# A transformer block on one core: the written order kept for TensorE, VectorE and ScalarE to the end of the kernel

## The chip, the cores and the metric

The kernel runs on one core of a Trainium2 chip. A core has five instruction streams that run side by side and wait for each other by semaphores: TensorE (PE: matmuls; its weight loads are listed as PEld), VectorE (DVE), ScalarE (ACT), GpSimd (POOL) and SyncE (SP), which here only issues DMAs. Each stream executes its instructions in the order in which they stand. The metric is the device time of one execution in microseconds (us).

## The reference

The input is one sequence of 2048 rows of 640 floats. An attention block is followed by a gated MLP whose gate mixes rows:

```python
h  = x + _A_ref(_layernorm(x), wqkv, wo)     # 32 heads of 20, window of 256 rows
z  = gelu(layernorm(h) @ w_in)               # 640 -> 1728
z1 = z[..., :864]
z2 = layernorm(z[..., 864:])
g  = einsum("ts,bsf->btf", w_sp, z2) + b_sp  # 2048 x 2048 matrix over the rows
h2 = h + (z1 * g) @ w_out                    # 864 -> 640
```

All is float32. The kernel keeps that precision on TensorE by splitting each operand into a high part and a low rest and adding three products.

## The kernel before

The sequence is cut into 16 tiles of 128 rows. After attention, whose part of the program ends at line 657, the kernel goes through these stages:

1. **Output projection** (`for i in range(NT)`, 16 tiles). `norm_o` (L148, DVE) divides the attention output by the softmax sums, `split_o` (L156 a copy on ACT, L157 a subtraction on POOL) splits it, `proj_o` (L91, PE, 30 matmuls) multiplies it by `wo`, L1160 (DVE) adds the input, `layernorm` takes statistics (L75, L76 on DVE), the power on POOL (L77, L78), and scales on DVE (L81). `turn_h` (L806) transposes the result two tiles later. The sums come from `inverse_sums` (L348, a reciprocal on DVE of what a DMA, L345, has loaded). Meanwhile `win1_prep` splits the first half of `w_in` a few pieces per tile: copies on ACT (`zl<-wraw`), subtractions on DVE and POOL.
2. **z1**: eight `z_pair`s of 8 products each (L866), with Strassen-like sums of operands, so seven products in place of eight.
3. **z2, first half**: four `z2_pair`s, two tiles each, four products of 15 matmuls (L917). After the gelu on ACT (L921) come statistics on DVE (L939, L941), the power on POOL (L942, L943), the scaling on DVE (L947), and `right_blocks`: sums and splits of four blocks into seven pieces (`ze`, `zl`), high parts by ACT (L681), low parts by DVE and POOL (L675, the line of the helper `plus`).
4. **First gates**: eight `gate_pair`s of 7 products of 12 matmuls (L1013) of `w_sp` with the seven pieces of all four pairs; `w_sp` tiles are loaded into `fx` and split into `aw`.
5. **z2, second half**, and 6. **second gates**: the same with the other half of the rows; in the second gates each product is followed by transposes (L1041) and the last projection (L1052) of earlier tiles, and `w_out` is loaded and split in the first two of them (L124, L125).

Stages 2 to 6 are written as a list `steps`, one product each, and a table `later` of work that `at(n, f)` hangs on a step. `run(n)` emits, in this order, what hangs on step n, the product of step n, and the reading of its bank:

```python
    def run(n):
        for f in later.pop(n, []):
            f()
        if 0 <= n < len(steps):
            steps[n][0]()
            steps[n][1]()
```

Buffers are written out: four PSUM banks with the tag `a` and four with `b`, four rows, two halves of `fx`.

What sets the order of instructions on an engine is the scheduler of the framework, which by default reorders each engine's instructions as far as data allow, by its own estimate of when each would be ready. A context, `manual_schedule(engines=...)`, holds the listed engines to the order in which the program emits them. It is entered at the top for PE, DVE and ACT and held in the stack `ms`; line 657, `ms.close()`, leaves it. So in the kernel before attention runs in the written order, and all that follows in the scheduler's. POOL is never held; SP is held only inside a part of attention.

Of the kernel before, what the change touches and what calls it, by code (L numbers as in the profile page):

```python
# [34 lines left out]
def block_kernel(ctx, tc, x, wqk, wv, wo, w_in, wsp, bsp, w_out, out):  # L35
    nc = tc.nc
    ms = ctx.enter_context(ExitStack())
# [616 lines left out]
                pass  # L654


    ms.close()
    psK = ctx.enter_context(ExitStack())

    def acc_tile(name):  # L660
# [555 lines left out]
```

## Time and profile before

| | us |
|---|---|
| median of 3 runs | 1148.1 |
| lowest and highest | 1143.98, 1149.98 |
| span of the profiled execution | 1144.7 |

The profile page gives the profiled execution by its span, 3.4 us under the median. In what follows a row of the timeline gives start, duration, engine, line, operation, output and inputs, count, and in brackets the idle time before it with what ended it; a row of the windows gives, for a stretch of the span, the busy time of each engine (instructions in brackets), the granted clock of TensorE (1.00 is full) and the share of DMA. A row of groups gives busy time and mean ns of one, then the idle time before. The busy time of PE counts pipelined matmuls, so a busy PE at half clock looks as busy as at full clock; rates are therefore taken from start to start.

### The profile page before, as it was taken

Reading aid. Unit: us, or ns where it says so; the run is one execution under the profiler, and the core shown is the slowest. Engines: PE = TensorE matmul, PEld = TensorE weight load, DVE = VectorE, ACT = ScalarE, POOL = GpSimd, SP = SyncE. Lnnn points to the kernel's source line nnn. Section 1 sums busy time; section 2 is a strip of 40 time slices with the busy share of each in tenths; the row PEclk is TensorE's granted clock in tenths of the full one; section 3 lists DMA queues with packets and bytes.
Section 4 is the critical chain, followed back from the end, with each engine's and each line's share of the span. In section 5 each row is a group of like instructions: output and inputs, shape, how many; then the busy total and the mean of one; then the engine's idle time right before and its main releaser. Section 6 shows DMA issues by size and latency. Waiting matters only on the chain. (4 is left out here: it accounts for less than half of the span.)

```text
span 1144.7 us, 27633 instructions
## 1 busy us (share of the span) xinstructions
PE 1096.0 (96%) x10652; PEld 983.2 (86%) x10652; DVE 746.7 (65%) x1963; ACT 535.8 (47%) x1165; POOL 405.5 (35%) x553
## 2 busy tenths in 40 slices
PE   6999999999999999888999998999999899999998
PEld 6998887668788786788999997999999799999998
DVE  5541113789999996599677588455558974556543
ACT  3333433259999899344266554333334421222210
POOL 4124444547777678376220263000126410000000
PEclk9999999999999999899999998999999999999999
DMA  6212565656666635588455411323331463344322
GB/s 196 70 36 94 169 217 175 211 185 196 203 203 215 200 119 181 177 273 280 181 178 179 164 59 38 102 102 124 123 112 53 162 214 117 122 145 136 107 71 80
DMA packets 83844, 170.84 MB, mean 149 GB/s; under 512 B 11008, under 2 KB 47360, under 8 KB 79872
## 3 DMA queue, kind: packets, MB, share of 16 engines
q1 hardware_dynamic: 81408, 163.83, 44.3%
q10 hardware_dynamic: 2304, 5.24, 1.2%
q8 instruction: 83, 1.36, 0.5%
q14 instruction: 49, 0.40, 0.1%
HBM read 112.37 MB, written 56.23 MB: 147 GB/s over the span
## 5 line engine op out<-in xcount | busy, mean ns | idle before, releaser
L369 ACT ACTIVATE pt<-bank 128x384 f32<-128x384 f32 (+2 forms) x512 | 201.6, 496 | 13.9 <-PE bank L366 10.2
L1013 PE MATMUL g<-zl,aw 128*128 128x432 f32 x768 | 174.4, 362 | 7.3 <-ACT zl L681 4.9
L681 ACT ACTIVATE aw<-fx 128x512 fp32r<-128x512 f32 (+2 forms) x160 | 92.7, 595 | 187.6 <-PE g L1013 120.7
L312 DVE CUSTOM_DVE_ANT_0 junk<-bank,strip 128x288 bf16<-128x288 f32 x392 | 157.3, 454 | 6.6 <-PE bank L300 3.7
L1013 PEld LDWEIGHTS g<-zl,aw 128*128 128x128 f32 x768 | 144.8, 189 | 16.3 <-ACT zl L681 5.9
L1013 PE MATMUL g<-ze,aw 128*128 128x432 f32 x576 | 138.1, 368 | 6.0 <-DVE row L675 3.8
L675 DVE TENSOR_TENSOR aw<-fx,aw 128x512 fp32r<-128x512 f32 (+2 forms) x152 | 108.6, 723 | 37.2 <-ACT aw L681 36.7
L394 PE MATMUL pv<-pt,v_sb 128*32 128x192 f32 (+3 forms) x1984 | 126.8, 322 | 4.2 <-POOL pt L371 2.4
L1013 PEld LDWEIGHTS g<-ze,aw 128*128 128x128 f32 x576 | 109.2, 192 | 13.8 <-issue 3.2
L366 PE MATMUL bank<-slot 123*32 123x288 bf16 (+6 forms) x1536 | 107.0, 282 | 2.1 <-ACT pt L369 1.1
L371 POOL TENSOR_SCALAR_AFFINE_SELECT pt<-pt 128x512 f32<-128x512 f32 x128 | 84.0, 657 | 48.7 <-ACT pt L369 47.9
L1052 PE MATMUL out_ps<-wout,y_sp 128*128 128x320 f32 (+1 forms) x630 | 96.2, 310 | 0.4 <-ACT y_sp L124 0.4
L1052 PEld LDWEIGHTS out_ps<-wout,y_sp 128*128 128x128 f32 (+1 forms) x630 | 94.1, 188 | 1.3 <-ACT y_sp L124 0.7
L917 PE MATMUL zb<-win,aw 128*128 128x432 f32 x480 | 95.2, 359 | 0.0
L917 PEld LDWEIGHTS zb<-win,aw 128*128 128x128 f32 x480 | 90.0, 188 | 4.5
L300 PE MATMUL bank<-slot 120*32 120x288 bf16 (+2 forms) x1264 | 89.6, 286 | 0.0
L498 DVE TENSOR_TENSOR rest<-qk,sg 128x512 f32<-128x512 f32 x40 | 27.7, 691 | 85.7 <-ACT sg L496 85.7
L675 DVE TENSOR_TENSOR row<-g,row 128x432 f32<-128x432 f32 x80 | 48.0, 603 | 38.0 <-PE g L1013 32.5
L374 POOL TENSOR_SCALAR_AFFINE_SELECT pt<-pt 128x512 f32<-128x512 f32 x112 | 72.3, 645 | 0.0
L501 POOL TENSOR_TENSOR sg<-rest,sg 128x512 bf16<-128x512 f32 x40 | 46.6, 1164 | 72.1 <-ACT sg L500 68.9
L394 PEld LDWEIGHTS pv<-pt,v_sb 128*32 128x32 f32 x1984 | 59.4, 110 | 10.5 <-POOL pt L371 4.5
L366 PEld LDWEIGHTS <-slot 123*32 123x32 bf16 x1536 | 52.6, 97 | 17.2 <-issue 6.0
(189 smaller groups left out, 2172.7 us busy)
## 6 DMA issues: line engine op xcount, KB each, us to landing
fx<-wsp_in SPq DMA_DIRECT2D x32, 512.0 KB
slot<-qk_d SPq DMA_DIRECT2D x72, 200.0 KB
qk_d<-sg SPq DMA_DIRECT2D x32, 384.0 KB
slot<-qk_d SPq DMA_DIRECT2D x72, 160.0 KB
fx<-hn_d SPq DMA_DIRECT2D x32, 320.0 KB
o_d<-ot SPq DMA_DIRECT2D x64, 128.0 KB
z_d<-row SPq DMA_DIRECT2D x16, 432.0 KB
g_d<-row SPq DMA_DIRECT2D x16, 432.0 KB
```

Of the source, the lines that this page charges most:

```text
L300: nc.tensor.matmul(ps[32 * j:32 * j + 32, :n], part(st, half, 120, 0, hh, q0, 32), part(st, half, 120, 1, hh, lo + skip * j, n), start=Tru ...
L312: nc.vector.tensor_tensor_reduce(out=junk[:, :n], in0=ps[:, :n], in1=keep, scale=1.0, scalar=NEG, op0=OP.add, op1=OP.max, accum_out=m_cols ...
L366: nc.tensor.matmul(ps[32 * i:32 * i + 32, b:e], part(st, half, 123, 1, hh, k0, 32), part(st, half, 123, 0, hh, kb * P + b, e - b), start=T ...
L369: nc.scalar.activation(pt[:, hh, :n], ps[:, :n], AF.Exp, scale=SCALE)
L371: nc.gpsimd.affine_select(out=pt[:, :, :P], in_=pt[:, :, :P], pattern=[[0, 4], [1, P]], base=0, channel_multiplier=-1, compare_op=OP.is_ge ...
L374: nc.gpsimd.affine_select(out=pt[:, :, 256:], in_=pt[:, :, 256:], pattern=[[0, 4], [-1, P]], base=-1, channel_multiplier=1, compare_op=OP. ...
L394: nc.tensor.matmul(ps[32 * hh:32 * hh + 32, a - 512 * c:b - 512 * c], v_sb[:, kb, v0:v0 + 32], pt[:, hh, a - kb * P:b - kb * P], start=fir ...
L675: (eng or nc.vector).tensor_tensor(out=out, in0=a, in1=b, op=op)
L681: nc.scalar.activation(out, a, AF.Copy)
L917: nc.tensor.matmul(b[0][:, :HF], a[t][:, x, kk], win2[0][:, y, kk, h * HF:(h + 1) * HF], start=kk + x + y == 0, stop=kk == KD - 1 and x == 1)
L1013: nc.tensor.matmul(ps, w[m][:, x, k], zc[k][m][:, y], start=start and k + x + y == 0, stop=stop and k == 3 and x == 1, skip_group_check=True)
L1052: nc.tensor.matmul(ps[j][:, :HD], src[:w, a, k, :], e1["wout"][:w, b, k, j * HD:(j + 1) * HD], start=(k == 0 and a + b == 0), stop=(k == K ...
```

## The change

Line 657 goes; nothing else changes. The context now ends with the function, so PE, DVE and ACT keep the written order through stages 1 to 6. The work, the buffers and their sizes are the same.

```diff
@@ -654,7 +654,7 @@
                 pass
 
 
-    ms.close()
+
     psK = ctx.enter_context(ExitStack())
```

POOL and SP are still ordered by the scheduler, whose estimates now start from another order on the three engines, so their rows move too. TensorE changes least: within the second gates its products, transposes and projections alternate much as they did. Three places show what moves. Names stand with the number of the buffer; `inv` is the tile of sums, `m` holds attention output (and the normalised rows that L81 writes), `xh` the rows of the input, `st` and `mv` statistics.

VectorE where attention ends and the output projection begins, before:

```order
L148 TENSOR_TENSOR m_8920<-m_8920 128x5x128 x3
L154 CAST t_8919<-m_8920 128x640
L157 TENSOR_TENSOR t_8919<-m_8920,t_8919 128x640
L348 RECIPROCAL inv_9398<-inv_9398 128x128
L1160 TENSOR_TENSOR xh_8921<-wo_ps_9473,xh_8921 128x640
L75 BN_STATS stc_9608<-xh_8921 128x6 x2
L76 BN_AGGR mvc_9609<-stc_9608 128x2
L81 TENSOR_SCALAR m_8920<-xh_8921,mvc_9609 128x640
L1160 TENSOR_TENSOR xh_8922<-wo_ps_9518,xh_8922 128x640
L75 BN_STATS stc_9624<-xh_8922 128x6 x2
L148 TENSOR_TENSOR m_8920<-m_8920 128x5x128 x2
L348 RECIPROCAL inv_9549<-inv_9549 128x128
```

The same place now:

```order
L148 TENSOR_TENSOR m_8920<-m_8920 128x5x128
L154 CAST t_8919<-m_8920 128x640
L157 TENSOR_TENSOR t_8919<-m_8920,t_8919 128x640
L348 RECIPROCAL inv_9398<-inv_9398 128x128
L348 RECIPROCAL inv_9549<-inv_9549 128x128
L148 TENSOR_TENSOR m_8920<-m_8920 128x5x128
L1160 TENSOR_TENSOR xh_8921<-wo_ps_9473,xh_8921 128x640
L75 BN_STATS stc_9607<-xh_8921 128x6 x2
L76 BN_AGGR mvc_9608<-stc_9607 128x2
L81 TENSOR_SCALAR m_8920<-xh_8921,mvc_9608 128x640
L148 TENSOR_TENSOR m_8920<-m_8920 128x5x128
L1160 TENSOR_TENSOR xh_8922<-wo_ps_9518,xh_8922 128x640
```

The last reciprocal, `inv_9549`, has moved ahead of the normalising of tile 2 and of the adds of tiles 0 and 1, and from there on one tile's add, statistics and scaling stand in one piece, with one normalising between tiles.

ScalarE in the same stretch, before (`osp` and the `t` of L156 are the high parts of the projection's operand, `zl` those of `w_in`, `ho` the transposed rows, the DMA stores the sum to `h_d`):

```order
L156 ACTIVATE osp_9569<-m_8920 128x640
L156 ACTIVATE t_8919<-m_8920 128x640
L408 ACTIVATE ot_3_0_9512<-pv_3_9347 128x256
L408 ACTIVATE ot_3_1_9515<-pv_3_9347 128x256
L1161 DMA h_d<-xh_8921 128x640
L1161 DMA h_d<-xh_8922 128x640
```

Now:

```order
L408 ACTIVATE ot_3_0_9512<-pv_3_9347 128x256
L408 ACTIVATE ot_3_1_9515<-pv_3_9347 128x256
L1161 DMA h_d<-xh_8921 128x640
L156 ACTIVATE osp_9568<-m_8920 128x640
L1161 DMA h_d<-xh_8922 128x640
L681 ACTIVATE zl_9572<-wraw 128x432
L156 ACTIVATE t_8919<-m_8920 128x640
L681 ACTIVATE ho_8923<-ht_ps_9673 128x640
L1161 DMA h_d<-xh_9565 128x640
L681 ACTIVATE zl_9574<-wraw 128x432
L156 ACTIVATE t_8919<-m_8920 128x640
```

The copy of tile 2 (`osp`) stands behind the store of tile 0, and later copies also behind high parts of `w_in`.

VectorE at the end of the first z2 half, from the scaling of the last tile on (`row` holds z2, `zl` takes its pieces, `aw` the split `w_sp` of the first gates, `fx` and `tmp` its sums), before:

```order
L947 TENSOR_SCALAR row_9591<-row_9591,mvz_0_11571 128x864
L675 TENSOR_TENSOR zl_9577<-row_9589,zl_9577 128x432
L675 TENSOR_TENSOR aw<-fx,aw 128x512
L675 TENSOR_TENSOR zl_9582<-row_9591,zl_9582 128x432
L675 TENSOR_TENSOR aw<-fx,aw 128x512
L939 BN_STATS stz_1_11620<-row_9592 128x6
L675 TENSOR_TENSOR row_9591<-row_9591 128x432
L675 TENSOR_TENSOR fx<-fx 128x512
L941 BN_AGGR mvz_1_11621<-stz_1_11620 128x2
L675 TENSOR_TENSOR zl_9583<-row_9591,zl_9583 128x432
L675 TENSOR_TENSOR aw<-fx,aw 128x512
L947 TENSOR_SCALAR row_9592<-row_9592,mvz_1_11621 128x864
```

The last tile's scaling and what follows it now:

```order
L947 TENSOR_SCALAR row_9591<-row_9591,mvz_1_11620 128x864
L675 TENSOR_TENSOR row_9590<-row_9591,row_9590 128x432 x2
L675 TENSOR_TENSOR zl_9584<-row_9591,zl_9584 128x432
L675 TENSOR_TENSOR zl_9583<-row_9590,zl_9583 128x432
L675 TENSOR_TENSOR zl_9586<-row_9591,zl_9586 128x432
L675 TENSOR_TENSOR row_9591<-row_9591,row_9590 128x432
L675 TENSOR_TENSOR zl_9585<-row_9590,zl_9585 128x432
L675 TENSOR_TENSOR zl_9587<-row_9591,zl_9587 128x432
L675 TENSOR_TENSOR aw<-fx,aw 128x512
L675 TENSOR_TENSOR fx<-fx 128x512
L675 TENSOR_TENSOR aw<-fx,aw 128x512 x3
```

The gate's own splits (`aw<-fx`), which stood between the statistics and the scaling, now stand behind all pieces of the last pair.

## The prediction

> **What bounds the kernel now.** I read the page's busy shares first, then the windows by stage, then the waits of PE, then the timelines of single engines where PE waits. The change touches nothing before about 465 us. The windows of what it touches, in the order projection, z1, z2 first half, start of the first gates, first gates, z2 second half, start of the second gates, second gates:
>
> ```profile
> 481.00:563.00 82.00, 73.50 (x496) 71.22 (x495) 73.65 (x120) 29.26 (x52) 46.00 (x48) 0.98 0.77 256
> 563.00:644.00 81.00, 81.00 (x420) 77.43 (x419) 55.19 (x101) 51.50 (x96) 12.91 (x8) 1.00 0.52 175
> 644.00:696.00 52.00, 52.00 (x266) 49.54 (x265) 39.68 (x60) 25.25 (x48) 27.95 (x29) 1.00 0.21 72
> 696.00:719.00 23.00, 18.02 (x74) 15.48 (x73) 19.87 (x31) 11.19 (x22) 6.30 (x6) 0.85 0.15 46
> 719.00:831.00 112.00, 111.19 (x565) 105.54 (x564) 57.74 (x91) 40.49 (x73) 4.33 (x3) 1.00 0.34 115
> 831.00:886.00 55.00, 54.95 (x280) 52.12 (x279) 38.19 (x60) 24.17 (x46) 25.89 (x28) 1.00 0.26 86
> 886.00:911.00 25.00, 19.92 (x89) 17.41 (x88) 23.93 (x36) 11.16 (x20) 12.14 (x8) 0.93 0.50 167
> 911.00:1124.00 213.00, 210.62 (x1261) 204.14 (x1260) 119.27 (x216) 44.29 (x89) 7.89 (x5) 1.00 0.41 129
> ```
>
> After the lengths come PE, PEld, DVE, ACT, POOL, then the clock. PE is the bound with no gap in z1 and z2 and nearly none in the gates. It loses time in three places: the projection (82.0 - 73.5 = 8.5), and the starts of both gates. A matmul there takes 0.197:
>
> ```profile
> 650.63 45.05 PE L917 MATMUL zb<-win,aw 128*128 128x432 f32 x228
> 695.52 1.35 PE L1013 MATMUL g<-ze,aw 128*128 128x432 f32 x6
> ```
>
> so the 74 matmuls of 696 to 719 are 14.6 us of work in 23, a loss of 8.4, and the 89 of 886 to 911 are 17.5 in 25, a loss of 7.5; both hold idle time and a lower clock. In these three places DVE is busy 90%, 86% and 96%: there the order on DVE sets the pace. All an ordering could win is 8.5 + 8.4 + 7.5 + 0.8 + 2.4, some 28 us.
>
> **Term A, the projection.** In the written order the last reciprocal stands ahead of the normalising of tile 2. Before:
>
> ```profile
> 469.07 7.22 PE L91 MATMUL wo_ps<-t 128*128 128x320 f32 x30 [4.09 <-DVE t L154]
> 481.20 4.57 PE L91 MATMUL wo_ps<-t,osp 128*128 128x320 f32 x30
> 557.49 4.65 PE L91 MATMUL wo_ps<-t 128*128 128x320 f32 x30
> 562.44 1.43 PE L866 MATMUL zv<-zl,aw 128*128 128x432 f32 x6
> 482.26 0.51 SPq L345 DMA_DIRECT2D inv<-o_d  x1
> 485.48 1.56 DVE L148 TENSOR_TENSOR m<-m 128x640 f32<-128x640 f32 x2 [2.34 <-DMA inv<-o_d]
> 486.96 0.95 DVE L348 RECIPROCAL inv<-inv 128x128 f32<-128x128 f32 x1
> 473.88 1.56 POOL L157 TENSOR_TENSOR osp<-m,osp 128x640 fp32r<-128x640 f32 x1 [8.81 <-DMA wraw<-w_in_in]
> ```
>
> The DMA for the reciprocal was issued at 482.26 and landed at about 485.4. Now the reciprocal runs at 485.4 to 486.4, then the normalising (0.8), then tile 0's add (0.8); ACT's copy of tile 2 follows the store of tile 0 (from 488), and POOL's subtraction (1.56) ends near 490.8. So TensorE starts tile 2 at about 490 and not at 481.2. From there PE alone would need 14 tiles of 562.44 - 557.49 = 4.95, which is 69.3, and end at 560.1, 2.3 before the 562.44 it ended at: that is the lower end. But DVE is nearer to the bound. A tile alone on DVE already shows the written pattern at the end of this stage:
>
> ```profile
> 557.74 0.82 DVE L1160 TENSOR_TENSOR xh<-wo_ps,xh 128x640 f32<-128x640 f32 x1
> 558.59 0.89 DVE L75 BATCH_NORM_STATS2 stc<-xh 128x6 f32<-128x320 f32 x2
> 559.51 0.21 DVE L76 BATCH_NORM_AGGREGATE mvc<-stc 128x2 f32<-128x12 f32 x1
> 560.71 0.61 DVE L81 TENSOR_SCALAR m<-xh,mvc 128x640 f32<-128x640 f32 x1 [0.99 <-POOL mvc L78]
> 565.16 0.61 DVE L81 TENSOR_SCALAR m<-xh,mvc 128x640 f32<-128x640 f32 x1 [0.99 <-POOL mvc L78]
> ```
>
> Between L76 and L81 DVE waits 0.99 for POOL. The scheduler filled that wait with other tiles' work; now it is bare, with the next tile's work queued behind it: 16 x 0.99 = 15.8. The work left at 486.4 is the 73.65 of the window, less the reciprocal (0.95), plus what had been done by 481 (tile 0's 0.82 + 0.89 + 0.21 + 0.61, two normalisings, 4.1) and what came after 563 (1.7): 78.5. Then the last L81 ends at 486.4 + 78.5 + 15.8 = 580.7, where it ended at 565.8: +14.9. Part of the 78.5 is time in which DVE stood behind POOL:
>
> ```profile
> L81 DVE TENSOR_SCALAR m<-xh,mvc 128x640 f32<-128x640 f32 x15 | 14.4, 957 | 5.5 <-POOL mvc L78 4.5 <-PE wo_ps L91 1.0
> L675 DVE TENSOR_TENSOR zl<-wraw,zl 128x432 fp32r<-128x432 f32 x10 | 9.4, 957 | 0.0
> 489.67 1.84 DVE L81 TENSOR_SCALAR m<-xh,mvc 128x640 f32<-128x640 f32 x1 [1.01 <-POOL mvc L78]
> 494.84 0.55 DVE L675 TENSOR_TENSOR zl<-wraw,zl 128x432 fp32r<-128x432 f32 x1
> ```
>
> L81 takes 957 ns on average and 0.61 alone, zl 957 and 0.55: 15 x 0.35 + 10 x 0.41 = 9.3 of excess, which a DVE that waits anyway may not pay: +5.6. On the other side POOL's new order puts a subtraction (1.1 to 1.6) between its two steps of the power in six of the 16 tiles, about 8 us more of waiting: +22.9 at the upper end. ACT's copies now also queue behind high parts of `w_in` that wait for DVE. I take +12, between +5.6 and +22.9 and nearer the two DVE sums than the lower end of -2.3. [...]
>
> **Term C, the start of the first gates.** The gates need the pieces of all four z2 pairs. In the trace the first pair's scalings on DVE and the last tile's are
>
> ```profile
> 657.36 0.53 ACT L921 ACTIVATE row<-zb 128x432 f32<-128x432 f32 x1 [0.29 <-PE zb L917]
> 658.41 0.20 DVE L941 BATCH_NORM_AGGREGATE mvz<-stz 128x2 f32<-128x12 f32 x1
> 658.53 0.55 DVE L939 BATCH_NORM_STATS2 stz<-row 128x6 f32<-128x432 f32 x1
> 659.60 0.73 DVE L947 TENSOR_SCALAR row<-row,mvz 128x864 f32<-128x864 f32 x1 [0.52 <-POOL mvz L943]
> 661.02 0.61 DVE L675 TENSOR_TENSOR ze<-row,ze 128x432 fp32r<-128x432 f32 x1 [0.69 <-ACT ze L681]
> 665.15 0.73 DVE L947 TENSOR_SCALAR row<-row,mvz 128x864 f32<-128x864 f32 x1 [0.52 <-POOL mvz L943]
> 674.89 0.73 DVE L947 TENSOR_SCALAR row<-row,mvz 128x864 f32<-128x864 f32 x1 [0.46 <-POOL mvz L943]
> 705.95 0.73 DVE L947 TENSOR_SCALAR row<-row,mvz 128x864 f32<-128x864 f32 x1 [0.46 <-POOL mvz L943]
> 667.70 1.71 POOL L675 TENSOR_TENSOR aw<-fx,aw 128x640 fp32r<-128x640 f32 x1 [0.19 <-ACT aw L681]
> 709.44 2.15 DVE L675 TENSOR_TENSOR zl<-row,zl 128x432 fp32r<-128x432 f32 x4
> ```
>
> Within the pair 5.55 passed; in the written order the second wait for an ACT copy (0.69) is bare too: 6.3. From there to the next pair's scaling 9.74 passed, the length of POOL's two sums and two rests ahead of the next power; POOL's 1.71 for `aw` now stands ahead of this stretch: 8.0. A pair then takes 14.3, the chain from the first scaling to the last 3 x 14.3 + 6.3 = 49.2, plus about 1.5 for gate splits between; it was 705.95 - 659.60 = 46.35. The first scaling comes 30 matmuls (5.9) and a gelu, statistics and the power (657.36 to 659.60: 2.3) after the stage's start: 8.2. After the last one DVE now does the scaling, eight pieces at 0.54 and four of the gate's own splits at about 0.6 before PE can go on with the fourth product: 7.4, and then 46 matmuls (9.1) end the first pair. Sum 8.2 + 49.2 + 1.5 + 16.5 = 75.4, against 240 + 84 matmuls without a gap, 63.8: a loss of 11.6, where 8.4 was lost: +3.2. Ends: with the old chain of 46.35 and no splits between, -1.1; with POOL's 9.74 unchanged (3 x 1.74 more), +8.4.
>
> **Term E**, the start of the second gates, is the same with 7.5 lost before: +4.1, from -0.2 to +9.3.
>
> **Term F, second gates.** Before, the last pair's PE waited once for a row of g that came late by DMA:
>
> ```profile
> 1103.11 1.42 PE L1013 MATMUL g<-ze,aw 128*128 128x432 f32 x6 [1.84 <-DVE row L675]
> ```
>
> In the written order DVE reads a bank right behind each product. Its work per pair, some 20 us (119.27 over 213 is 56%), lies under 30 of PE; the tightest place, the seventh product, which waits for an add two products earlier, has some 0.4 to spare. I take -2, from -2.4 to +3. `w_out`'s splits, through one row at a time, are the risk. z1 and the first gates go at nothing: PE covers DVE's 55 of 81 and 58 of 112; if the cover were gone, each bare POOL or ACT wait would cost 0.7 to 1.0.
>
> Sum: 12 + 3.2 + 4.1 - 2 = +17.3. The profiled span 1144.7 becomes 1162; the median of the runs stands 3.4 above that span: 1165.
>
> **The rivals.** *Heavier*: PE waits for POOL's rest, which waits for ACT's copy behind a high part of `w_in`, which waits for DVE, whose add waits for PE; a cycle of waits rather than a sum of DVE work. With the upper ends of A, C and E and no gain in F it is +41: 1189. For it speak the rows of ACT in the new order, against it that ACT is busy only 29 of 82.
> *Covered*: POOL's pieces fall into DVE's waits, A is +5.6, C -1.1, E -0.2, F -2: +2.3, 1150, no change.
> *Faster*: the scheduler put gate splits (`aw<-fx`) between the last z2 statistics and the last scaling, which PE needs; the written order does not. If a pair takes under 13.3, C turns to a gain; at 12 it is 8.2 + 42.3 + 16.5 - 63.8 = 3.2 lost, -5.2 in C and -4.3 in E; with -2.3 in A and -2 in F the time is 1134. Against it speaks POOL's 9.74, which no order on DVE shortens.
> *Clock*: the row of 469.07 shows 30 matmuls in 7.22 after 4.09 of idling, 4.65 elsewhere, so a long gap costs 2.6 more; I count none, because PE then waits for DVE again. With three such gaps counted, 1173, inside the forecast. [...]
>
> **Chances.** Forecast (1156 to 1177, with the clock) 0.58; heavier 0.16; covered 0.16; faster 0.10. 0.5%, about what a measurement here can tell, is 5.7 us: slower 0.76, no change 0.15, faster 0.09. The range leaves out most of the faster case and the far end of the heavier one: 1147 to 1187.
>
> **What would show it.** A: tile 2's projection starts near 490, DVE shows an idle 1.0 or more before each L81, z1's first product starts near 574. C and E: the eight L947 come in pairs 6 and 8 apart; PE stops once for 5 to 8 us in the first gate product and again in the third and fourth. F: no stall longer than 0.5 after 930. I am wrong if z1 starts before 566 or if L947 goes through in 46 or less.

## The result, and the profile after

The changed kernel takes 1201.2 us at the median of four runs, against 1146.0 for the kernel before: the ratio is 1.049, with a 95% interval of 1.0468 to 1.0512. That is 55 us slower. The forecast was 1165, the range ended at 1187, and the dearest rival stood at 1189.

The profiled execution spans 1199.3, which is 54.6 more than before. Its windows by stage come first: projection from tile 2 on, z1, z2 first half, first gates in two pieces, z2 second half, second gates in two pieces.

```profile
487.50:581.80 94.30, 80.08 (x491) 76.56 (x491) 66.50 (x106) 27.70 (x46) 43.25 (x52) 0.90 0.63 210
581.80:673.60 91.80, 87.46 (x445) 81.60 (x443) 64.92 (x119) 53.52 (x104) 12.81 (x9) 1.00 0.49 166
673.60:734.20 60.60, 52.02 (x241) 48.38 (x241) 37.22 (x57) 24.64 (x47) 30.54 (x33) 0.92 0.19 60
734.20:764.00 29.80, 24.80 (x115) 22.73 (x114) 22.06 (x37) 13.69 (x26) 0.79 (x2) 0.89 0.27 89
764.00:874.10 110.10, 110.10 (x561) 105.08 (x561) 53.55 (x85) 37.36 (x67) 2.91 (x2) 1.00 0.32 112
874.10:935.30 61.20, 51.50 (x242) 47.86 (x241) 37.15 (x56) 24.26 (x47) 28.87 (x31) 0.92 0.20 62
935.30:988.00 52.70, 43.14 (x210) 39.98 (x209) 38.64 (x58) 18.32 (x35) 14.04 (x9) 0.90 0.50 157
988.00:1179.00 191.00, 190.74 (x1146) 185.30 (x1145) 105.61 (x194) 36.02 (x76) 0.00 (x0) 1.00 0.39 126
```

Where the gates run alone, TensorE is full (110.10 of 110.10, 190.74 of 191.00), as it nearly was before (111.19 of 112.00, 210.62 of 213.00). The loss is in z2, which had no gap before and now takes 60.6 and 61.2 for 47.3 of matmuls, and in the projection. The timeline of TensorE shows the places:

```profile
487.53 1.44 PE L91 MATMUL wo_ps<-t,osp 128*128 128x320 f32 x4 [7.24 <-ACT osp L156]
581.78 1.43 PE L866 MATMUL zv<-zl,aw 128*128 128x432 f32 x6
673.62 12.35 PE L917 MATMUL zb<-win,aw 128*128 128x432 f32 x62
686.82 12.09 PE L917 MATMUL zb<-win,aw 128*128 128x432 f32 x60 [0.85 <-DVE aw L675]
702.34 14.57 PE L917 MATMUL zb<-win,aw 128*128 128x432 f32 x60 [3.42 <-DVE aw L675]
721.21 13.19 PE L917 MATMUL zb<-win,aw 128*128 128x432 f32 x58 [4.31 <-DVE aw L675]
734.24 1.35 PE L1013 MATMUL g<-ze,aw 128*128 128x432 f32 x6
744.15 2.53 PE L1013 MATMUL g<-ze,aw 128*128 128x432 f32 x6 [5.00 <-ACT row L681]
935.28 1.35 PE L1013 MATMUL g<-ze,aw 128*128 128x432 f32 x6
970.77 2.50 PE L1013 MATMUL g<-ze,aw 128*128 128x432 f32 x6 [4.80 <-DVE row L675]
989.14 0.86 PE L1013 MATMUL g<-ze,aw 128*128 128x432 f32 x3 [0.26 <-DVE row L675]
```

Start to start, against before, and against 0.197 for each matmul without a gap:

| term | how it is read | us |
|---|---|---|
| A, projection | z1's first product at 581.78, was 562.44 (6.3 at tile 2's start, 13.0 behind it) | +19.3 |
| z1 | 581.78 to 673.62 is 91.8; before, 562.44 to 695.52 less 47.3 of z2 is 85.8 | +6.1 |
| C, z2 first half | 60.6, less 47.3 | +13.3 |
| C, first gates | 7.4 lost (139.8 less 132.4), was 10.1 | -2.7 |
| E, z2 second half | 61.2, less 47.3 | +13.9 |
| E, start of the second gates | the rest of 935.28 to 989.14 (53.9, was 48.65) | -1.2 |
| F, second gates | the stop at 970.77: 4.80, and 1.6 of slow matmuls (granted clock 0.68 from 970.77 to 976) | +6.4 |
| F, behind 989 | to the end | -0.5 |

The sum is 54.6. In z2 each pair of tiles but the first begins with a wait for the low part of its own operand `aw`, written by DVE (18.3 in six waits over both halves). DVE's scalings of z2 set the pace, as the experiments below bear out:

```profile
682.12 0.73 DVE L947 TENSOR_SCALAR row<-row,mvz 128x864 f32<-128x864 f32 x1 [1.00 <-POOL mvz L943]
697.64 0.73 DVE L947 TENSOR_SCALAR row<-row,mvz 128x864 f32<-128x864 f32 x1 [1.00 <-POOL mvz L943]
716.52 0.73 DVE L947 TENSOR_SCALAR row<-row,mvz 128x864 f32<-128x864 f32 x1 [0.99 <-POOL mvz L943]
734.04 0.73 DVE L947 TENSOR_SCALAR row<-row,mvz 128x864 f32<-128x864 f32 x1 [1.58 <-POOL mvz L943]
740.22 0.73 DVE L947 TENSOR_SCALAR row<-row,mvz 128x864 f32<-128x864 f32 x1 [0.99 <-POOL mvz L943]
```

These are the first scaling of each pair, and the last of all. The pairs are 15.5, 18.9 and 17.5 apart, and the chain from first to last is 58.1, where it was 46.35. What DVE waited for in z2's first half, before (644 to 711) and after (673.6 to 745), from the waits of DVE:

```profile
DVE aw L675 <- ACT aw L681: 7.8, 5, 5.7
DVE row L947 <- POOL mvz L943: 3.2, 5, 1.2
DVE ze L675 <- ACT ze L681: 0.7, 1, 0.7
DVE stz L939 <- ACT row L921: 0.6, 1, 0.6
DVE zl L675 <- ACT zl L681: 0.2, 1, 0.2
```

```profile
DVE stz L939 <- ACT row L921: 10.9, 5, 2.9
DVE row L947 <- POOL mvz L943: 8.6, 8, 1.6
DVE zl L675 <- ACT zl L681: 2.9, 5, 0.7
DVE ze L675 <- ACT ze L681: 2.6, 4, 0.7
```

The columns after the colon are total, count and longest; waits for TensorE (1.4 before, 0.6 after) are left out. Some of these waits lie ahead of the first scaling: 6.6 of the 7.8 for `aw` before, and after it 5.2 of the 10.9, for the gelus of the first products. Between the first scaling and the last, DVE's rows hold 4.7 of waits before and 18.6 after: 7.6 for powers, 5.7 for gelus, 5.3 for high parts. That is 13.9 more, in a chain that is 11.8 longer. In the projection, from 487.5 to 581.8, DVE is busy 66.5 and waits 26.3, together 92.8 of the 94.3:

```profile
DVE m L81 <- POOL mvc L78: 21.7, 14, 2.5
DVE xh L1160 <- PE wo_ps L91: 4.6, 2, 3.2
```

### The profile page after: what moved, and what is told of

It reads as the page before. It is cut to its first block, busy times and chain, and to the rows that moved or that the text cites. A ratio compares the mean times of both kernels' runs of the same rounds, so it can differ in the third digit from the quotient of the medians.

```text
span 1199.3 us, 27549 instructions
## 1 busy us (share of the span) xinstructions
PE 1113.7 (93%) x10652; PEld 996.7 (83%) x10652; DVE 743.8 (62%) x1963; ACT 533.0 (44%) x1165; POOL 391.7 (33%) x553
## 4 chain that ended last, share of the span: by engine, by line
PE 65%; DVE 11%; issue 7%; POOL 6%; ACT 5%; DMA 4%; SPq 2%; POOLq 0%; ACTq 0%; DVEq 0%
PE g L1013 20%; PE out_ps L1052 8%; PE pv L394 6%; PE bank L300 5%; PE bank L366 5%; PE qk L482 2%; PE zx L866 2%; PE qk L484 2%; PE qk L483 2%; DVE zl L675 1%; PE zy L866 1%; PE zv L866 1%; DMA qk_d<-sg 1%; ACT aw L681 1%; PE v L458 1%
## 5 line engine op out<-in xcount | busy, mean ns | idle before, releaser
L1013 PEld LDWEIGHTS g<-zl,aw 128*128 128x128 f32 x768 | 147.4, 192 | 7.4
L675 DVE TENSOR_TENSOR aw<-fx,aw 128x512 fp32r<-128x512 f32 (+2 forms) x152 | 105.2, 707 | 26.2 <-ACT aw L681 26.0
L917 PE MATMUL zb<-win,aw 128*128 128x432 f32 x480 | 103.9, 379 | 18.3 <-DVE aw L675 18.3
L917 PEld LDWEIGHTS zb<-win,aw 128*128 128x128 f32 x480 | 96.3, 202 | 25.6 <-DVE aw L675 20.5
L366 PE MATMUL bank<-slot 123*32 123x288 bf16 (+5 forms) x1536 | 107.2, 283 | 2.3 <-ACT pt L369 1.4
L498 DVE TENSOR_TENSOR rest<-qk,sg 128x512 f32<-128x512 f32 x40 | 27.7, 692 | 86.2 <-ACT sg L496 86.2
L91 PE MATMUL wo_ps<-t 128*128 128x320 f32 x330 | 59.5, 341 | 16.8 <-POOL t L157 7.2
L91 PEld LDWEIGHTS wo_ps<-t 128*128 128x128 f32 x330 | 55.0, 212 | 20.1 <-POOL t L157 8.9
```

Of the source, the lines that this page charges most:

```text
L91: nc.tensor.matmul(ps[:, j, :n], a(k), b(k, j), start=(k == 0 and a is lh and b is rh), stop=(k == ks - 1 and a is ll))
L366: nc.tensor.matmul(ps[32 * i:32 * i + 32, b:e], part(st, half, 123, 1, hh, k0, 32), part(st, half, 123, 0, hh, kb * P + b, e - b), start=T ...
L675: (eng or nc.vector).tensor_tensor(out=out, in0=a, in1=b, op=op)
L917: nc.tensor.matmul(b[0][:, :HF], a[t][:, x, kk], win2[0][:, y, kk, h * HF:(h + 1) * HF], start=kk + x + y == 0, stop=kk == KD - 1 and x == 1)
L1013: nc.tensor.matmul(ps, w[m][:, x, k], zc[k][m][:, y], start=start and k + x + y == 0, stop=stop and k == 3 and x == 1, skip_group_check=True)
```

## The experiments

Each kernel ran in three rounds against the kernel before. Lines added ahead of a stage raise its line numbers by a few. "Changed" is the changed kernel (ratio 1.049).

### Which part of the program: order held for the projection alone, and from z1 on alone

```diff
 # e1_proj, on the changed kernel
+    ms.close()
     w2p = None
     for n in range(len(steps)):
```

> The written order is held through the output projection and given up ahead of z1. In the profile of the changed kernel z1's first product comes 19.3 us later (581.8 against 562.4) and the rest of the 54.6 us is lost behind it: 19.4 more up to the first gate product, 11.2 to the second gates, 4.7 to the end. Theory, the stages' losses are separate and add up: z1 starts near 581 to 582, everything behind it takes as long as before, and the time is about 19 us over before, near 1165. Rival, the stages are coupled: the scheduler makes the lateness good under the matmuls of z1 and z2 (then clearly under 1160), or the projection's lateness is what starves z1 and z2, and then the time is near 1190 even with the order given up.

```diff
 # e2_gates, on the kernel before
+    ms.enter_context(tc.manual_schedule(engines={PE, DVE, Activation}))
     w2p = None
     for n in range(len(steps)):
```

> The scheduler has the output projection as before, and the written order is held again from z1's first product to the end. Theory, separate losses: the projection keeps its 82 us, z1's first product comes near 562, and about 35 us are lost behind it: near 1181. PE waits for the low parts of z2's operand (L917 behind DVE aw L675) six times for 18 us in all, as in the changed kernel. Rival, coupled stages: with the projection undisturbed, z1 and z2 start with more work done ahead and lose less than half of that: 1165 or less.

The ratios are 1.0283 (1.0251 to 1.0315) for e1_proj and 1.0316 (1.0287 to 1.0344) for e2_gates: 32 and 36 us. e2_gates came as the theory had it: 17.2 of PE's waits for `aw`, and z1 takes 91.0 (559.5 to 650.5) although the projection was undisturbed, so z1's loss is its own and not the projection's lateness. e1_proj was missed by 13, and not in the rival's way either: the gates and the second half took no longer than before, but the projection took 99.2 and not 94.3, and z1 and z2 together 8 more than before (141.3, was 133.1). The order of that kernel's rows suggests why the first: the scheduler, free behind the projection, moved z1's splits (`aw<-fx`, `fx<-fx`) forward between the add, the statistics and the scaling of its tiles on DVE, the engine that is short there, and DVE waits 6.7 for ACT's copies of `aw` among them (5.0 in one wait). The two parts add up to 68, not to 55: where the order is given up costs too.

### Which engine: one held at a time

```diff
 # e3_dve, e4_act, e5_pe, on the kernel before
     ms.close()
+    ms.enter_context(tc.manual_schedule(engines={DVE}))  # or {Activation}, or {PE}
```

> After attention only VectorE keeps the written order; TensorE and ScalarE are the scheduler's. Theory, a cycle of waits through two queues: in z2 PE waits for a low part of the next operand (DVE), which stands behind statistics that wait for a gelu (ACT), which stands behind a copy that waits for POOL's sum; DVE's bare waits for POOL's power and for ACT's copies are there with DVE alone, the late gelus only with ACT held too. So DVE alone loses most but not all: +25 to +40, 1172 to 1187. Rival, DVE alone is the whole of it: within 3 of the changed kernel, 1198 to 1204. Rival, only all three together hurt: under 1160.

> After attention only ScalarE keeps the written order. Theory: ACT is busy 35% of these stages and has room, so its order alone costs what its late gelus and copies cost where DVE is tight: +5 to +15, 1152 to 1162. Rival, ACT's queue is what the cycle needs (copies of one pair ahead of gelus of the next): +25 or more. Rival, nothing: within 3 of before.

> After attention only TensorE keeps the written order. DVE alone cost 64 us and ACT alone 91 (1206.2 and 1232.8 against 1142.1), more than all three together. Theory, an engine held alone waits for work that the scheduler put late on the others, and pays more the more partners it has per product: PE alone then costs as well, +10 to +40, but least of the three, since its products stood nearly in the written order before. Rival, PE's order is free: within 4 of before.

DVE alone gives 1.0555 (1.0518 to 1.0591), ACT alone 1.0786 (1.0756 to 1.0816), PE alone 1.0106 (1.0076 to 1.0135). DVE alone and ACT alone each cost more than all three together (64 and 90 us against 55), and both theories were too low. For ACT the rival's range, 25 or more, holds; its cause is not shown by that. PE alone costs 12, the low end of its theory. The timeline of TensorE in e4_act shows one case, which comes back in every pair of z1 but the first:

```profile
601.67 3.61 PE L867 MATMUL zv<-zl,aw 128*128 128x432 f32 x9 [3.81 <-ACT tmp L682]
```

The scheduler's PE goes on with a product of the `v` bank, which is waiting to be read by ACT (`tmp<-zv`); ACT in the written order comes to that copy only behind another copy, which waited 4.69 for a sum on DVE, and two gelus. The wait is 3.81, and the nine matmuls behind it take 3.61 in place of 1.92. With PE held too, that wait is not there. So these runs do not split the 55 us by engine; they say that a mix of the two orders can cost more than either order kept for all three engines.

### The projection: what paces it

Four runs change what stands in one row. In e8_head tile 2's normalising and split stand ahead of the last reciprocals:

```diff
+        norm_o(2, nc.vector)
         for f in inverse:
             for _ in f:
                 pass
 ...
+        if i == 0:
+            split_o(2, nc.gpsimd)
```

> The changed kernel with the normalising and the split of tile 2 moved ahead of the last reciprocals and of tile 0's add, as the scheduler had it. Theory, DVE paces the projection: PE starts tile 2 some 6 earlier (481 and not 487.5), but DVE's row behind the reciprocal is only one normalising (0.8) shorter, so z1's first product comes 1 to 3 earlier. Rival, the late start of tile 2 is passed on whole: 6 to 7 earlier.

In e9_fill the normalising stands between statistics and scaling:

```diff
-        if i + 2 < NT:
-            norm_o(i + 2, nc.vector)
+        if i == 0:
+            norm_o(2, nc.vector)
 ...
-        layernorm(hn(i), xt, D, f"c{i}")
+        layernorm(hn(i), xt, D, f"c{i}", lambda: norm_o(i + 3, nc.vector) if i + 3 < NT else None)
```

> The changed kernel with one thing moved: in the projection the normalising of the tile after next is written between statistics and scaling, where DVE waited for POOL's power. Theory of the prediction, DVE's bare waits set the stage's pace: 14 waits of 1.0 are filled with 0.8, z1's first product comes 8 to 11 earlier than 581.8. Rival, ACT's queue sets it: PE waits for ACT's copies (13.5 in all) and for POOL's subtraction behind them (7.8), because the copies stand behind high parts of w_in, which wait for DVE's sums; then 0 to 4.

In e10_wtop the pieces of `w_in` stand at the top of a tile:

```diff
+        next(w1, None)
+        if i % 2:
+            next(w1, None)
         run(i - NT)
 ...
         layernorm(hn(i), xt, D, f"c{i}")
-        next(w1, None)
-        if i % 2:
-            next(w1, None)
```

> The changed kernel with one thing moved: the pieces of w_in are written at the top of each tile of the projection, behind the normalising, and not behind the layer norm. On ACT the projection's copy then stands ahead of the high parts of the same tile, and on DVE the sum that a high part waits for stands ahead of the add. Theory, ACT's queue behind w_in sets the pace: the waits of PE for ACT's t and POOL's subtraction (6.3 and 7.2) fall by more than half, with the half clock behind them 6 to 12 earlier. Rival, DVE's bare waits set it: no change, within 3.

None of the three can be told from the changed kernel: 1.0472 (1.0423 to 1.0521), 1.0456 (1.0413 to 1.0498), 1.0460 (1.0416 to 1.0505). In e8_head tile 2 starts at 480.3 and z1 at 577.9, so of 7.2 won at the head 3.9 arrive (attention itself ends some us earlier or later: without this edit tile 2 starts between 485.1 and 491.7). In e10_wtop PE's waits change places (ACT's `t` 3.5, was 6.3, and `osp` 8.7, was 7.2; POOL's subtractions 9.8, was 7.8) and the stage takes 93.6, was 94.3: ACT's queue behind `w_in` is not the pace. In e9_fill the stage takes 91.9, 2.4 less where the theory had 8 to 11. GpSimd's rows in the changed kernel and in e9_fill, at the same tile, say why:

```profile
493.14 0.22 POOL L77 TENSOR_SCALAR mvc<-mvc 128x1 f32<-128x1 f32 x1 [3.38 <-DVE mvc L76]
493.44 0.57 POOL L78 TENSOR_TENSOR mvc<-mvc,half 128x1 f32<-128x1 f32 x1
```

```profile
493.30 0.82 POOL L77 TENSOR_SCALAR mvc<-mvc 128x1 f32<-128x1 f32 x1 [2.63 <-DVE mvc L76]
494.20 0.57 POOL L78 TENSOR_TENSOR mvc<-mvc,half 128x1 f32<-128x1 f32 x1
```

The normalising on DVE ran from 493.21 to 494.03, and POOL's sum beside it took 0.82 in place of 0.22: the filling held up what it was to hide.

The next run fills the wait with the add and the statistics of the next tile, by writing the scaling one tile later. Its first form, e12_lagp, left the load of `x` where it was; that load overwrites what the late scaling reads, so most tiles scale a row of another tile.

```diff
-        layernorm(hn(i), xt, D, f"c{i}")
+        scales.append([])
+        layernorm(hn(i), xt, D, f"c{i}", later=scales[-1])
+        if i:
+            scales[i - 1].pop()()
 # g1_lagp also:
-        for n in (2, 3, 4) if i == 0 else (i + 4,) if i + 4 < NT else ():
+        for n in (2, 3, 4) if i == 0 else ():
             load_x2(n)
 ...
+            if i + 4 < NT:
+                load_x2(i + 4)
```

> The changed kernel with the scaling of the projection's layer norm written one tile later, behind the next tile's add and statistics, so that DVE does these while POOL takes the power. With the normalising as the filling only 2.4 were won in the stage (94.3 to 91.9): in that run L77 on POOL took 0.68 to 0.82 in place of 0.22 beside DVE's product of two SBUF operands. Add and statistics read one SBUF operand at most. Theory, DVE's waits for POOL's power (21.7 of 94.3) are what paces the stage: they fall to 5 or less and the stage gets 12 to 16 shorter, near 80. Rival, ACT's and POOL's queues pace it behind DVE: PE's waits for copies and subtractions stay, and the stage gets at most 5 shorter.

> Again the scaling of the projection's layer norm one tile later, now with the load of x that overwrites its source written behind it as well (in the run before it stood ahead, and DVE waited 18.1 for that load, so that run says nothing on the power). Theory, DVE's waits for POOL's power (21.7 of the stage's 94.3) are its pace: they go, the stage gets 12 to 16 shorter, near 80, the kernel 10 to 15 below the changed one. Rival, POOL's and ACT's rows behind DVE are the pace: the stage gets at most 5 shorter.

e12_lagp (1.0493, 1.0447 to 1.0539) shows nothing on the power, since its scaling waited 18.1 for that load. g1_lagp gives 1.0427 (1.0406 to 1.0448), 7 us under the changed kernel. DVE's waits in the projection (485 to 585) are now

```profile
DVE xh L1167 <- PE wo_ps L97: 20.1, 9, 4.6
DVE m L82 <- POOL mvc L78: 1.0, 2, 0.8
```

The waits for the power are gone as the theory said, 21.7 to 1.0, but the stage takes 86.2 (485.6 to 571.9), 8.1 less and not 12 to 16. The rest of the wait turned into one for TensorE's products; TensorE itself waits for POOL's subtractions (7.1) and runs at a granted clock of 0.90. So the bare waits were the pace, with a second limit 8 below them.

In g2_nowin the pieces of `w_in` are written behind the projection (the three `next(w1, None)` lines are left out; what is not done in the loop is done after it).

> The changed kernel with the pieces of w_in written behind the projection and not within it, so that z1 starts late; what counts is the projection alone, from tile 2's first product to the end of its last (94.3 less the last tile's transposes in the changed kernel). Without the pieces DVE has 4.3 per tile with the bare wait (0.82 + 0.82 + 0.89 + 0.21 + 0.61 + 0.99), TensorE 4.95. Theory, in the written order pieces and tiles add up on DVE and POOL: the projection falls to TensorE's 70 to 74. Rival, the chain of one tile (norm, copy, subtraction, product, add, power, scaling) is the pace: 84 or more.

From tile 2's first product to the end of the last the stage falls from 93.9 to 80.8, between the two expectations: the pieces cost 13, and 11 stay over TensorE's 70. DVE's own row still fills the stage, without a wait for TensorE: it is busy 56.7 and waits 22.9 for the power, 79.6 of the 80.8. The expectation gave it 4.3 per tile, with 0.61 for the scaling and 0.99 for the wait; the scaling took 1.22 on average, and the 14 waits 1.6. The kernel itself is slower (1.0596, 1.0577 to 1.0616), since z1 has to wait for the pieces.

### z2: where the wait shows, and what it hangs on

e6_prep writes the split of z2's operand one product earlier. e13_lagz does that too, and for the first three pairs of a half writes scaling and pieces one product later, behind the next statistics.

```diff
 # e6_prep
-            at(m - (1 if soon else 3), lambda t=t: prep(t, True, None))
-            at(m - (1 if soon else 2), lambda t=t: prep(t, False, nc.gpsimd if t else nc.vector))
+            at(m - (1 if soon else 4), lambda t=t: prep(t, True, None))
+            at(m - (1 if soon else 3), lambda t=t: prep(t, False, nc.gpsimd if t else nc.vector))
 # e13_lagz also, for k < 3
-        at(n0 + 2, lambda: (stat(0, 1), norm(0), f[0](), f[1](), f[2]()))
-        at(n0 + 3, lambda: stat(1, 0))
-        at(n0 + 4, lambda: (stat(1, 1), norm(1), f[3]()))
-        at(n0 + 5, lambda: (f[4](), f[5](), f[6]()))
+        at(n0 + 2, lambda: stat(0, 1))
+        at(n0 + 3, lambda: (norm(0), f[0](), stat(1, 0)))
+        at(n0 + 4, lambda: (f[1](), f[2](), stat(1, 1)))
+        at(n0 + 5, lambda: (norm(1), f[3]()))
+        at(n0 + 6, lambda: (f[4](), f[5](), f[6]()))
```

> The changed kernel with one thing moved: the split of z2's operand (copy on ACT, subtraction on DVE or POOL) is written one product earlier, so that on DVE it stands ahead of the statistics, the scaling and the pieces of the pair before. Theory, in z2 PE waits for that split because it is queued behind scaling and pieces, which wait for gelu, power and copies: the six waits of L917 for aw (18.3 us) and the half clock behind them (some 9 us) go, a part comes back as waiting for the last pieces at the gates: 12 to 18 less than the changed kernel, 1183 to 1189 on its scale. Rival, DVE's in-order work per pair is the period whatever stands first in it: the wait moves to the third gate product, where 5.0 is lost already, and less than 5 are won.

> The changed kernel with z2's operand split written one product earlier (as in the run above, which moved PE's wait but not the end: the chain of scalings L947 went from 58.1 to 55.8 only, 46.35 before the change) and, for the first three pairs of each half, scaling and pieces written one product later, behind the next statistics. Theory, DVE's bare waits are the pace: it waited 9.5 for the power, 7.7 for gelus and 5.6 for copies in z2 with the split moved, 4.7 in all before the change; with the power and the copies covered the chain of L947 falls to 47 to 50 and the kernel gets 12 to 18 shorter than the changed one. Rival, ACT's late gelus (behind copies that wait for POOL's sums) are the pace: DVE waits for gelus instead, and less than 6 are won.

e6_prep gives 1.0476 (1.0433 to 1.0519), which cannot be told from the changed kernel: the theory behind it fell, and the rival's account holds. z2's products took 53.1 (677.2 to 730.3), 7.5 less, but the gates stop where the last pieces are late:

```profile
736.82 1.73 PE L1013 MATMUL g<-zl,aw 128*128 128x432 f32 x3 [4.47 <-ACT zl L681]
745.49 1.45 PE L1013 MATMUL g<-ze,aw 128*128 128x432 f32 x6 [3.80 <-ACT row L681]
```

The first and the last scaling of e6_prep and of e13_lagz are

```profile
685.74 0.73 DVE L947 TENSOR_SCALAR row<-row,mvz 128x864 f32<-128x864 f32 x1 [1.00 <-POOL mvz L943]
741.56 0.73 DVE L947 TENSOR_SCALAR row<-row,mvz 128x864 f32<-128x864 f32 x1 [1.00 <-POOL mvz L943]
```

```profile
687.66 0.73 DVE L947 TENSOR_SCALAR row<-row,mvz 128x864 f32<-128x864 f32 x1 [2.26 <-POOL mvz L943]
739.37 0.73 DVE L947 TENSOR_SCALAR row<-row,mvz 128x864 f32<-128x864 f32 x1 [1.00 <-POOL mvz L943]
```

The chain is 55.8 in e6_prep and 51.7 in e13_lagz, after 58.1. e13_lagz gives 1.0424 (1.0378 to 1.0469), some 8 us under the changed kernel, less than the 12 to 18 expected, as the chain was to fall to 47 to 50. Inside its chain no wait for a gelu is left (5.7 in the changed kernel) and 3.6 for high parts (5.3), but the power, which was to be covered, is still waited for 7.1 (7.6). Over both halves the chains of the two runs got 4.5 and 12.5 shorter, for some 2 and 8 us. The time goes with the chain of scalings on DVE, not with the wait that PE shows in z2.

### The wait by itself

g3_pow_after and g4_pow_before take POOL's sum ahead of each power of the projection and of z2 four times. The place in z2 is shown; the helper `layernorm` has the same loop for the projection's tiles.

```diff
-                nc.gpsimd.tensor_scalar(out=mv[:, 2:3], in0=mv[:, 1:2], scalar1=EPS, scalar2=None, op0=OP.add)
+                for _ in range(4):
+                    nc.gpsimd.tensor_scalar(out=mv[:, 2:3], in0=mv[:, 1:2], scalar1=EPS, scalar2=None, op0=OP.add)
```

> The changed kernel with POOL's sum ahead of each power of the projection and of z2 taken four times, about 0.9 more for each of the 32 powers (the result is the same). Theory, in the written order each wait for a power lies bare on the path: the 16 of the projection and the 8 of each half of z2 cost nearly all of it, +22 to +30 over the changed kernel. Rival, other queues pace these stages: +12 or less.

> The same four-fold sum in the kernel before. Theory, the scheduler has other work in DVE's row while a power is taken: +10 or less, under half of what the changed kernel pays. Rival, the powers are as bare there, and both pay the same.

g3_pow_after gives 1.0761 (1.0734 to 1.0788), 31 over the changed kernel; g4_pow_before gives 1.0126 (1.0108 to 1.0144), 14 over the kernel before. Four sums take 1.09 in place of 0.22, so the 32 powers got 28 us longer: the written order pays all of it, the scheduler's half.

```profile
501.82 1.09 POOL L78 TENSOR_SCALAR mvc<-mvc 128x1 f32<-128x1 f32 x4 [3.38 <-DVE mvc L76]
```

In the written order it is paid where the powers are: from start to start the projection and z1 together took 13.1 longer (16 powers, 13.9), the first half of z2 and its gates 7.5, and the second half up to the first product of the last projection 6.6 (8 powers each, 7.0). So these powers lie bare on the path there. The edit lengthens POOL's row too; that the wait on DVE is what counts is shown for the projection by g1_lagp, which moves only DVE's scaling and the load of `x`. The runs also say that the powers are not free in the kernel before, where 10 or less was expected. The waits for them in the projection, changed kernel's first (485 to 595, and 478 to 566):

```profile
DVE m L82 <- POOL mvc L79: 45.3, 14, 4.4
```

```profile
DVE m L82 <- POOL mvc L79: 6.6, 5, 1.9
```

In the changed kernel these waits grew by 23.6 (from 21.7) and the stage by 10.4: the scaling that follows took 613 ns on average with the longer sum, and 1224 without.

### The edits together, and under the scheduler

f1_all joins e8_head, e12_lagp and e13_lagz, and scales rows of another tile as e12_lagp does; f2_all joins e8_head, g1_lagp and e13_lagz; f3_sched puts the edits of g1_lagp and e13_lagz into the kernel before.

> The last three edits together. Theory, the losses are DVE's bare waits in separate stages: the gains of the three add up, the time is 25 to 35 under the changed kernel, some 20 to 30 over the kernel before (z1's 6, w_out's 6 in the second gates and the start of the gates remain). Rival, the stages hide one another's gains: less than two thirds of the sum.

> The changed kernel with three edits together: the normalising of tile 2 ahead of the reciprocals (alone some 2 less), the layer norm's scaling one tile later with the load of x behind it (alone some 8 less), z2's scalings and pieces one product later (alone some 8 less). Theory, DVE's bare waits lie in separate stages: the gains add up to 16 to 20, about 37 over the kernel before. Rival, one hides the other: under 12.

> The kernel before, order given up after attention, with the two later scalings (projection and z2) written in. The four-fold sum cost the kernel before 15 us, so half of its waits for the power lie on its path too. Theory, the scheduler orders by its own estimate and hides what it can wherever the lines stand: within 4 of before. Rival, the written place is what it starts from: 4 to 10 faster than before.

f1_all gives 1.0415 (1.0370 to 1.0461), 9 us under the changed kernel and not 25 to 35: e12_lagp had won nothing, and what is left is about what e8_head and e13_lagz won (2 and 8). f2_all gives 1.0265 (1.0227 to 1.0302), 26 us under the changed kernel, where the three alone won 2, 7 and 8, each uncertain by some 5: they add up at least. What f2_all still takes over the kernel before lies, by starts in the profiles, ahead of tile 2 (2.0), in the projection (4.9), in z1 (5.5), in the first half of z2 and its gates (6.1) and, for the largest part, from the second half to the first product of the last projection (14.7); these losses no run took apart. f3_sched gives 1.0000 (0.9979 to 1.0022): the scheduler finds the same time from either text. No version here beats the kernel before.

## Why the prediction was wrong

The sign and the kind of mechanism were right, the size was not: 17 us were forecast and 55 came.

- **A, +12 forecast, +19.3 measured.** The head came as told (tile 2 at 487.5, forecast 490, 481.2 before). The step that failed is the choice of 12, under the +14.9 of DVE's row, because some of its work was taken to be time behind POOL that need not be paid. The sum had 78.5 of work and 15.8 of waits; from the last reciprocal to the end of the last L81 (484.7 to 586.3) DVE was busy 72.1 and waited 28.3. It waited 23.7 for the power in 16 waits, since in six tiles POOL's order put a subtraction between sum and power, which the prediction kept for its upper end (+22.9), and 4.6 for TensorE, which the sum did not have. Of the excess only a part went: the pieces `zl` took 598 ns, were 957, but L81 took 1224, was 957. Eight of its 16 rows took 0.61 or 0.62, and eight 1.81 to 1.87, each of these just behind the start of a subtraction on POOL:

```profile
493.98 1.56 POOL L157 TENSOR_TENSOR t<-m,t 128x640 fp32r<-128x640 f32 x1
494.05 1.84 DVE L81 TENSOR_SCALAR m<-xh,mvc 128x640 f32<-128x640 f32 x1 [1.00 <-POOL mvc L78]
```

Beside the eight short rows POOL runs nothing. So the rows show that L81 took three times as long where a subtraction started just before it; what in the two instructions does that was not tried. g1_lagp shows that of the waits for the power some 8 are the stage's pace, and g2_nowin that the pieces of `w_in` are 13 of it.
- **z1 at nothing, +6.1 measured.** "PE covers DVE's 55 of 81" looked at shares. PE's waits in z1 are short, for ACT's copy of a bank (3.1 in five) and for the last two tiles' transposes (1.25). From start to start the five cost 4.4, some 0.27 each beyond the wait, and the transposes 1.6, which is nearly the whole. e2_gates has the same five waits (3.1) without a late projection; what holds that copy back in ACT's row was not tried.
- **C and E, +3.2 and +4.1 forecast, +10.6 and +12.7 measured.** This is the step that failed most: "a pair then takes 14.3", and the "about 1.5 for gate splits between". The stage's start came as told (8.5 for 8.2), but the chain took 58.1 and not 50.7. The first pair, with no gate split in it, took 15.5; at 1.2 for each of three pairs that is 3.6 of the error. The other two took 18.9 and 17.5, with rows of the gate's own work between (`aw` of 128x512 on DVE, `fx` on POOL): 5.4 in place of 1.5. The pair's length had been taken from rows of the scheduler's trace with two bare waits added. Left out were the waits for gelus (5.7 inside the chain), which are late because ACT, in its own written order, stands at a high part until POOL's sum is done; e13_lagz, without them, has a chain of 51.7. ScalarE's rows at the second pair:

```profile
694.15 0.57 ACT L681 ACTIVATE ze<-row 128x432 fp32r<-128x432 f32 x1 [1.79 <-POOL row L675]
694.62 0.72 ACT L681 ACTIVATE aw<-fx 128x640 fp32r<-128x640 f32 x1
695.25 0.51 ACT L921 ACTIVATE row<-zb 128x432 f32<-128x432 f32 x1
```

The gelu (L921) stands behind that copy, and DVE waited 2.35 for it. The prediction also had PE stop in the gate products only; in fact PE stopped ahead of each new pair in z2, because the split of its operand stands behind scaling and pieces on DVE. e6_prep shows that this second omission cost nothing by itself: moved, the stop turns up at the gates. The chain's length was the error.
- **Clock, none counted.** Behind the stops of z2 matmuls ran slow: 60 took 14.57 after 3.42 of waiting, at a granted clock of 0.81, and 12.09 after 0.85, at 1.00; 58 took 13.19 after 4.31, at 0.87. Against 0.201 for each, as in the 12.09 of 60, this is 2.5 and 1.5 within the first half's 13.3. But each of these stretches runs into the next stop (4.31 and 5.00), and behind the first pair the gelus wait only 0.2 for TensorE. A full clock would then have lengthened those stops: the prediction's reason, that PE waits for DVE again, held there as far as these rows tell. Behind the stop of 5.00, after which the gates run free, the slow clock does count: the 18 matmuls from 744.15 on took 5.9 from start to start, at a granted clock of 0.60, and would take 3.5 at 0.197 each. No run took the clock's part out. The rival's price of 2.6 for a gap was about the upper end, and its count of three was too small.
- **F, -2 forecast, +5.9 measured.** Behind 989 the written order is 0.5 better. The loss is the stop of 4.80 at 970.77. It lies where DVE waits for ACT's copies of the transposes, which stand behind splits of `w_sp` that had waited for a sum on DVE:

```profile
966.80 1.15 ACT L681 ACTIVATE aw<-fx 128x512 fp32r<-128x512 f32 x2 [3.09 <-DVE fx L675]
968.46 1.02 DVE L125 TENSOR_TENSOR y_sp<-yt_ps,y_sp 128x512 fp32r<-128x512 f32 x2 [1.76 <-ACT y_sp L124]
```

A copy for `w_out` had waited 3.53 for its load just before, so the risk that the prediction named, `w_out`'s splits through one row at a time, has a part in it; how much was not tried. (DVE's work per pair is 16.8 by the prediction's own share, 56% of 30, and not 20.)
- **The rivals.** *Heavier*, a cycle of waits, was nearest in time (1189) and in kind, but placed in the projection, where e10_wtop found no cycle through `w_in` on ACT. The rows above show a round of that kind in z2: DVE waits for a gelu, which stands behind a copy on ACT, which waits for a sum on POOL, which waits for DVE. e13_lagz took the waits for gelus out of it and won less than half of what z2 lost.

## What to carry to other kernels

A chain over several engines cannot be priced from a trace in which a scheduler had filled its waits: walk one round of it in the new order, engine by engine, with every wait of every queue it passes, and take the longest. A written order has to put work between an operation and its consumer on another engine, and work that does not hold up the operation it is meant to cover, as e9_fill's normalising did (0.82 in place of 0.22). An order held for one engine and left free on its partners can cost more than either whole.

## What the runs showed of the hardware

- POOL's sum of 128x1 (L77) took 0.21 or 0.22 in all 16 rows of the projection in the changed kernel. In e9_fill it took 0.68 to 0.82 in 11 of its first 15 rows there; in the eight of these up to 540 DVE's normalising (0.77 to 1.71) had started 0.09 to 1.0 before it. In a ninth row, where the two started together, it took 0.22.
- DVE's scaling of one tile (L81, 128x640) took 0.61 alone and 1.81 to 1.87 where a subtraction of 1.53 to 1.56 had started on POOL up to 0.07 before it, in eight of 16 rows of the changed kernel; beside the other eight POOL's timeline shows no instruction.
- The granted clock was lower behind some stops of TensorE. In the changed kernel it was 0.50 over the first 3.7 us behind the stop of 3.42 at 702.34, 0.81 over the 14.57 of the 60 matmuls there, and 1.00 over the 12.09 of the 60 behind the stop of 0.85. In the projection, 26 matmuls of 128x320 took 5.44 at 0.72 behind stops of 2.35 and 1.13 with four matmuls between them, and 4.08 at 1.00 behind a stop of 2.13. In e6_prep 28 matmuls took 7.31 behind a stop of 2.53 and 28 took 5.79 behind one of 0.42:

```profile
715.78 7.31 PE L917 MATMUL zb<-win,aw 128*128 128x432 f32 x28 [2.53 <-DVE aw L675]
724.64 5.79 PE L917 MATMUL zb<-win,aw 128*128 128x432 f32 x28 [0.42 <-POOL aw L675]
```
